# Seven half products for output tiles 0 and 1 in the steady cycles of a fused attention and MLP-mixer kernel

## The chip, the cores and the metric

The kernel runs on one core of a Trainium2 chip. Its engines work side by side, each through its own list of instructions in order: TensorE (PE, with its weight loads shown as PEld), VectorE (DVE), ScalarE (ACT), GpSimd (POOL) and SyncE (SP). DMAs are issued by SyncE, GpSimd and, in two places, ScalarE. The engines wait for one another through semaphores. The metric is the device time of one execution in microseconds; before and after are compared as medians of several runs.

## What is computed

```python
def _attn_ref(q, k, v):                      # q, k, v: 8 x 12 x 448 x 64
    scale = 1.0 / np.sqrt(q.shape[-1])
    scores = scale * np.matmul(q, k.transpose(0, 1, 3, 2)) - np.log(S)
    attn = 1.0 / (1.0 + np.exp(-scores))     # a sigmoid, no sum over keys
    return np.matmul(attn, v)

def _moe_ref(x, w_tok1, w_tok2, w_ch1, w_ch2):   # x: 8 x 448 x 768
    xt = x.transpose(0, 2, 1)
    h = np.maximum(xt @ w_tok1, 0.0) @ w_tok2    # 448 -> 256 -> 448, over tokens
    u = x + h.transpose(0, 2, 1)
    h2 = np.maximum(u @ w_ch1, 0.0) @ w_ch2      # 768 -> 1536 -> 768, over channels
    return u + h2                                # 8 x 448 x 768, fp32
```

The heads of the attention, side by side, are x. Everything is multiplied in fp16 and summed in fp32.

## The kernel before

A batch's twelve heads are handled as three *units* of four heads (u = 0, 1, 2), so that there are 24 *cycles*, c = 3b + u. In a cycle several stages of several batches stand side by side, in an order written out by hand (`tc.manual_schedule()`): what the Python program emits first stands first in each engine's list.

- *Scores*, `qk(b, u, j)` (L179): seven per unit. Four quarter products (64x64 weights, 448 columns) into a tile of two PSUM banks, then one sigmoid on ScalarE (L191). The tag `qk` has two such tiles, so the score after next waits for the sigmoid. The sigmoids' outputs `att` lie in ten buffers.
- *Values*, `av(b, u)` (L205), one cycle later: 28 quarter products into two banks; VectorE casts them to fp16 into `xTs[b % 2]` (L224), with a copy into the pad (L230). `xtrans_dma` (L239) then transposes x through a DMA on SyncE's queue into `xn`.
- *Token products*, `tok_tail`, `tok1` and `ytrans` (L264 to L333), two cycles later. `ytrans` ends with VectorE's add of x and the product into a tile of its own, `uts[b % 2]` (L323).
- In cycle 2 of batch b, `utrans(b - 1)` (L336) transposes u of the batch before through a DMA into `un`, `token_sums(b - 1)` forms four sums and differences of u (tile `diffs`), and `sevens(b - 1)` computes the first channel product as seven half products after Strassen and Winograd: `ORDER` (L1123) names each by its number and its column groups a, b, c, so that "5ab" is product 5 of groups a and b. They are accumulated in PSUM, and ScalarE moves some of them out to tiles of the ring `parts` (four buffers, L522 to L528); VectorE adds and clamps (L537, L540) into `h2`, of which there is one.
- *Second channel product* (`ch2...`), 448 tokens in four tiles (0 to 2 of 128 tokens, 3 of 64), two halves of 384 output channels, twelve blocks of 128 hidden channels. In cycle c of batch b it belongs to `lot` b - 2: `ch2_pair` for tile 0 in cycle 0 and tile 2 in cycle 2 (64 quarter and 8 full products each), and in cycle 1 `last_split` for tile 3 (48 quarters), `ch2_split` for the first half of tile 1 (48 quarters) and `ch2` for its second half (12 full). VectorE adds u from `un` into a tile `outs` (ring of three), which SyncE stores.
- `ch2_seven` (L723) does two output tiles at once by seven half products, six blocks each. It needs operand sums on both sides: `hsums`, sums of the weights `c2` made once by `output_sums` (L696, twelve VectorE instructions), and sums of `h2` per pair of tiles (`sums`, L750). Products 1, 6, 7 and 4 accumulate one after another in one bank ("X"), 5 and 3 in another; after each one VectorE adds the bank into the output tile (L790). Before the change it is used only in the last stage, for batches 6 and 7.
- `through_dma(b + 1)`: six VectorE copies (L126) and two DMA transposes (L139) bring the next batch's k and q into place; `some(n)` emits n of these pieces, `within` in the middle of a cycle and `behind` at its end. `gated_loads` issues the loads after next on GpSimd's queue, behind a copy that waits for the transposed q (L1048).

The loop of the steady cycles, L1209 to L1281, runs over b = 3 to 7. With "quarter" for a product of 64x64 weights and "full" for 128x128, its cycle reads, in TensorE's order:

```python
qk(b, u, 0); qk(b, u, 1); <quarters>; qk(b, u, 2)
av(*before, 0, 4); qk(b, u, 3); av(*before, 4, NJ); qk(b, u, 4)
<quarters>; qk(b, u, 5); <quarters>
tok_tail(*ahead); qk(b, u, 6); tok1(*ahead, with_scores=True)
<full products of ch2>; if u == 2: sevens(b - 1)
ytrans(*ahead)
```

Of the kernel before, what the change touches and what calls it, by code (L numbers as in the profile page):

```python
# [21 lines left out]
NJ = 7  # L22
NP = 64
NU = 3
# [6 lines left out]
def kernel(  # L31
# [44 lines left out]
    diffs = pc.tile([128, 4, NU, NS], FP16, name="diffs")  # L76
    xTs = [pc.tile([128, NU, 2, 512], FP16, name=f"xT{n}") for n in range(2)]

    uts = [pc.tile([128, NDB, 512], FP16, name=f"ut{n}") for n in range(2)]
# [125 lines left out]
    def av(b, u, j0=0, j1=NJ, banks=None):  # L205
        if j0 == 0:
            xa[b, u] = banks or [
                bank([128, 512], FP32, f"xa_{b}_{u}_{g}")
                for g in range(2)
            ]  # L210
        ps = xa[b, u]
        for j in range(j0, j1):
            for g in range(2):
                for hi in range(2):
                    nc.tensor.matmul(  # L215
                        out=ps[g][64 * hi : 64 * hi + 64, 0:S],
                        lhsT=raw[b, "v"][64 * g : 64 * g + 64, u, hi, j, :],
                        rhs=att[b, u, j][64 * g : 64 * g + 64, hi, :],
                        start=(j == 0),
                        stop=(j == NJ - 1),  # L220
                    )
        if j1 == NJ:
            for g in range(2):
                nc.vector.tensor_copy(  # L224
                    out=xTs[b % 2][:, u, g, 0:S], in_=ps[g][:, 0:S]
                )
            if NU * b + u >= N_CYCLES - 2:
                nc.vector.memset(xTs[b % 2][:, u, :, S:512], 0.0)
            elif NU * b + u >= N_FIRST:
                nc.vector.tensor_copy(  # L230
                    out=xTs[b % 2][:, u, :, S:512], in_=xTs[b % 2][:, u, :, S - 64 : S]
                )


    def xn_tile(b, u):
        xn[b, u] = pa.tile([128, 2, 4, 128], FP16, tag="xn", bufs=3, name=f"xn_{b}_{u}")
        return xn[b, u]

    def xtrans_dma(b, u):  # L239
        nc.sync.dma_start_transpose(  # L240
            out=xn_tile(b, u).rearrange("s g t d -> s (g t) d"),
            in_=xTs[b % 2][:, u, :, :].rearrange("d g s -> d (g s)"),
        )

    def xtrans(b, u):
        ps = bank([128, 4, 2, 128], FP16, f"xb_{b}_{u}")
        for g in range(2):
            for t in range(4):
                nc.tensor.transpose(
                    out=ps[:, t, g, :],  # L250
                    in_=xTs[b % 2][:, u, g, 128 * t : 128 * t + 128],
# [57 lines left out]
    def ytrans(b, u, banks=None):  # L309
# [11 lines left out]
        def add(g, ps):  # L321
            db = NU * g + u
            nc.vector.tensor_tensor(  # L323
                out=uts[b % 2][:, db, 0:S], in0=xTs[b % 2][:, u, g, 0:S], in1=ps[:, 0:S], op=ADD
            )
# [10 lines left out]
    def utrans(b):  # L336
        if b < B - 1:
            nc.vector.tensor_copy(
                out=uts[b % 2][:, 0:NU, S:512], in_=uts[b % 2][:, NU:NDB, S - 64 : S]
            )  # L340
        un[b] = pa.tile([128, NDB, 4, 128], FP16, tag="un", bufs=2, name=f"un_{b}")
        nc.sync.dma_start_transpose(
            out=un[b].rearrange("s db t d -> s (db t) d"),
            in_=uts[b % 2].rearrange("d db s -> d (db s)"),
# [6 lines left out]
    BY_UNIT = [NU * g + u for u in range(NU) for g in range(2)]  # L351

    def ch1(b, cb, d0=0, d1=NDB):
# [5 lines left out]
        for d in range(d0, d1):  # L359
# [3 lines left out]
                rhs=uts[b % 2][:, BY_UNIT[d], 0:S],  # L363
# [27 lines left out]
    def ch1_pair(b, cb):  # L391
# [3 lines left out]
        def step(turn, n):  # L395
# [7 lines left out]
                lambda p, part: uts[b % 2][part, BY_UNIT[n], 0:S],  # L403
# [34 lines left out]
    def token_sums(b, u0=0, u1=NU):  # L438

        ut = uts[b % 2]  # L440
        k1, k2 = slice(u0, u1), slice(NU + u0, NU + u1)
        n1, n2 = slice(0, NS), slice(NS, S)
        t1, t2, t3, t4 = (diffs[:, n, u0:u1, :] for n in range(4))
        for out, in0, in1, op in (
            (t1, ut[:, k1, n2], ut[:, k1, n1], SUB),
            (t3, ut[:, k2, n2], ut[:, k1, n2], SUB),
            (t2, t3, ut[:, k1, n1], ADD),
            (t4, ut[:, k2, n1], t2, SUB),
# [3 lines left out]
    def ch1_seven(b, banks):  # L452
# [3 lines left out]
        ut = uts[b % 2]  # L456
        s1, s2, s4 = sums
        low, high = slice(0, NU), slice(NU, NDB)
        n1, n2 = slice(0, NS), slice(NS, S)
        weights = {  # L460
# [9 lines left out]
            1: ut[:, low, n1],  # L470
            2: ut[:, high, n1],
            3: ut[:, high, n2],
            4: diffs[:, 3, :, :],
            5: diffs[:, 0, :, :],
            6: diffs[:, 1, :, :],
            7: diffs[:, 2, :, :],
# [71 lines left out]

    def ch2(b, t, half, n0=0, n1=NCB):
        cols = slice(DH * half, DH * half + DH)  # L550
        if n0 == 0:
            if half == 0:
                outs[b, t] = pa.tile([128, D], FP32, tag="outs", bufs=3, name=f"o_{b}_{t}")
# [12 lines left out]
        if b not in un:  # L566
            for n in range(NU):
                nc.tensor.matmul(
                    out=ps[:, 128 * n : 128 * n + 128],
                    lhsT=uts[b % 2][:, NU * half + n, 128 * t : 128 * t + 128],  # L570
# [6 lines left out]
    def ch2_out(b, t, half, ps):  # L577
        cols = slice(DH * half, DH * half + DH)
        if b in un:
            nc.vector.tensor_tensor(  # L580
                out=outs[b, t][:, cols].rearrange("s (u d) -> s u d", d=128),
                in0=un[b][:, NU * half : NU * half + NU, t, :],
# [5 lines left out]
        if half == 1:  # L588
# [9 lines left out]
    def ch2_pair(b, t):  # L598


        outs[b, t] = pa.tile([128, D], FP32, tag="outs", bufs=3, name=f"o_{b}_{t}")
# [47 lines left out]
    def ch2_split(b, t, half):  # L649

        outs[b, t] = pa.tile([128, D], FP32, tag="outs", bufs=3, name=f"o_{b}_{t}")
# [3 lines left out]
        def end():  # L655
            ch2_out(b, t, half, ps[0])
            o = outs[b, t][:, cols]
            nc.vector.tensor_tensor(out=o, in0=o, in1=ps[1][:, 0:DH], op=ADD)

# [9 lines left out]
    def last_split(b, ps):  # L669

        def end():
            o = pa.tile([128, DH], FP32, tag="outl", bufs=1, name=f"o_{b}_3")
# [3 lines left out]
                in0=un[b][:, 0:NU, 3, :],  # L676
# [19 lines left out]
    def output_sums():  # L696

        for tag in ("raw_k", "raw_q", "rel_k", "rel_q"):
            n = len(hsums) + 1
            hsums.append(  # L700
                pa.tile([128, NCB // 2, DH], FP16, tag=tag, bufs=1, name=f"hsum{n}")
            )
# [20 lines left out]
    class ch2_seven:  # L723
# [3 lines left out]
        def __init__(self, rows, sides, X, Y, Z):  # L727
            self.rows, self.ps, self.banks = rows, {}, {"X": X, "Y": Y, "Z": Z}
            b = rows[1][0]
            hid = pa.tile(  # L730
                [128, 3, NCB // 2, 128], FP16, tag="tr_k", bufs=2, name=f"hid_{b}"
            )
            hid3 = pa.tile([128, NCB // 2, 128], FP16, tag="tr_q", bufs=2, name=f"hid3_{b}")
            self.held = {n: hid[:, at, :, :] for at, n in enumerate((5, 6, 7))}
            self.held[3] = hid3[:, :, :]
            (self.a11, self.a12), (self.a21, self.a22) = [
                (side[:, LOW, :], side[:, HIGH, :]) for side in sides
            ]
            self.weights = {1: self.a11, 2: self.a12, 4: self.a22}
# [42 lines left out]

        def end(self, n):
            row, half = {1: (0, 0), 2: (0, 0), 6: (0, 1), 3: (0, 1)}.get(n, (1, int(n != 4)))
            b, t = self.rows[row]
            if (b, t) not in outs:
                outs[b, t] = pa.tile([128, D], FP32, tag="outs", bufs=3, name=f"o_{b}_{t}")
# [4 lines left out]
                in0=un[b][:, NU * half : NU * half + NU, t, :] if opens else o,  # L792
# [3 lines left out]
            if n in (3, 4):  # L796
                store(b, t)

    def ch2_last(b, n0=0, n1=NCB):
# [20 lines left out]
        for n in range(NU if add_on_pe else 0):  # L820
            for g in range(2):
                nc.tensor.matmul(
                    out=ps[g][:, 128 * n : 128 * n + 128],
                    lhsT=uts[b % 2][:, NU * g + n, 384:448],
# [4 lines left out]
        o = pa.tile([128, DH], FP32, tag="outl", bufs=1, name=f"o_{b}_3")  # L829
        for g in range(2):  # L830
# [4 lines left out]
            else:  # L835
                nc.vector.tensor_tensor(
                    out=o[parts[g], :].rearrange("s (u d) -> s u d", d=128),
                    in0=un[b][0:64, NU * g : NU * g + NU, 3, :],
# [30 lines left out]
    for n in range(2):  # L869
        nc.vector.memset(xTs[n][:, :, :, S:512], 0.0)  # L870
        nc.vector.memset(uts[n][:, :, S:512], 0.0)
# [254 lines left out]
    def sevens(b, banks=(2, 3, 0, 1, 0)):  # L1126
        step = ch1_seven(b, banks)
        for at, (n, gs) in enumerate(SEVENS):
            step(n, gs)
            if copies and at in (1, 3):  # L1130
# [77 lines left out]

    for c in range(ONE_RUN, N_CYCLES):  # L1209
        b, u = divmod(c, NU)  # L1210
        before, ahead = divmod(c - 1, NU), divmod(c - 2, NU)
        if b == NU:
            within, behind = ((0, 0), (3, 3), (2, 0))[u]
        else:
            within, behind = ((0, 2), (2, 4), (0, 0))[u] if b < B - 1 else (2, 2)
        if u == 0:
            assert not copies
            copies += through_dma(b + 1, 0) if b + 1 < B else output_sums()

        X, Y = 2, 0
        at_bank[0] = X
        if u == 1:
# [49 lines left out]
        if u == 2:  # L1274
            sevens(b - 1)
# [3 lines left out]
        if u == 1 and NU < b < B - 1:  # L1279
            gated_loads(b)  # L1280
# [38 lines left out]
    outs[B - 1, 2] = pa.tile([128, D], FP32, tag="raw_v", bufs=2, name=f"o_{B - 1}_2")  # L1319
# [57 lines left out]
```

## Time and profile before

| | |
|---|---|
| time, median of 3 runs | 344.02 us (343.84 to 344.08) |
| the profiled execution | 344.08 us, of which the profiled span is 342.3 us |
| granted TensorE clock, mean | 0.999 |
| busy: TensorE / VectorE / ScalarE / GpSimd | 335.2 / 219.1 / 214.3 / 56.7 us |
| batches 3 to 6 of the steady loop | 38.92 us each |
| output stores on SyncE's queue | 48 of 192 KB, 3.5 us to landing; 15 of 96 KB, 2.5 us |
| transposes on SyncE's queue, to landing | xn 3.5, tr_k 5.8, tr_q 6.5, un 9.3 us |

A line of the chain of waits gives a start in the span, a length, and the work that held the end of the kernel there, with the number of instructions merged into it. A line of the timeline gives the same for every engine, with the idle time ahead of it and what ended that in brackets. A line of the groups gives the busy time in all, the mean of one in ns, and the idle time of the engine before them. The output of a matmul is reported with a modelled end; a matmul overlaps its successor, so that a group's mean (some 320 ns for 384 columns) is longer than the time from one to the next. The line of the batches comes from the chain: the piece `PE c L383` that opens cycle 0 starts at 102.26, 141.19, 180.11, 219.03 and 257.95.

### The profile page before, as it was taken

Reading aid. Unit: us, or ns where it says so; the run is one execution under the profiler, and the core shown is the slowest. Engines: PE = TensorE matmul, PEld = TensorE weight load, DVE = VectorE, ACT = ScalarE, POOL = GpSimd, SP = SyncE. Lnnn points to the kernel's source line nnn. Section 1 sums busy time; section 2 is a strip of 40 time slices with the busy share of each in tenths; the row PEclk is TensorE's granted clock in tenths of the full one; section 3 lists DMA queues with packets and bytes.
Section 4 is the critical chain, followed back from the end, with each engine's and each line's share of the span. In section 5 each row is a group of like instructions: output and inputs, shape, how many; then the busy total and the mean of one; then the engine's idle time right before and its main releaser. Section 6 shows DMA issues by size and latency. Waiting matters only on the chain.

```text
span 342.3 us, 10437 instructions
## 1 busy us (share of the span) xinstructions
PE 335.2 (98%) x4543; PEld 238.9 (70%) x4543; DVE 219.1 (64%) x441; ACT 214.3 (63%) x272; POOL 56.7 (17%) x98
## 2 busy tenths in 40 slices
PE   7999999999999999999999999999999999999994
PEld 4556556555896669766896669766896669869862
DVE  2277466678774684666764674667655785876782
ACT  3997747388748785677648875577748876314200
POOL 8973440050040004000040004000100000000000
PEclk9999999999999999999999999999999999999999
DMA  7999999999999999998999599977991429029007
GB/s 124 164 177 194 207 204 204 157 170 177 243 170 209 161 141 202 193 172 133 184 189 187 113 181 168 226 127 137 188 191 33 100 57 163 2 54 181 7 6 201
DMA packets 104380, 52.17 MB, mean 152 GB/s; under 512 B 76432, under 2 KB 101264, under 8 KB 104336
## 3 DMA queue, kind: packets, MB, share of 16 engines
q1 hardware_dynamic: 78944, 29.70, 48.3%
q0 software_dynamic: 25168, 21.50, 41.6%
q8 instruction: 35, 0.57, 0.7%
q10 hardware_dynamic: 224, 0.33, 0.4%
q14 instruction: 9, 0.07, 0.1%
HBM read 43.45 MB, written 11.01 MB: 159 GB/s over the span
## 4 chain that ended last, share of the span: by engine, by line
PE 91%; ACT 5%; DMA 1%; DVE 1%; issue 1%; ACTq 0%; DVEq 0%
PE c_ab L507 14%; PE qk L184 10%; PE c_c L507 8%; PE c L383 8%; PE xa L215 8%; PE c L557 6%; PE c L772 6%; PE c L639 6%; PE tk L293 5%; PE yt L313 5%; ACT att L191 5%; PE c L621 4%; PE c L360 3%; DMA first_q<-in_q_dram 1%; PE c L811 1%; PE c_a L507 1%
## 5 line engine op out<-in xcount | busy, mean ns | idle before, releaser
L191 ACT ACTIVATE att<-qk,att_bias 128x896 f16<-128x896 f32 x168 | 157.2, 1014 | 42.2 <-PE qk L184 41.8
L184 PE MATMUL qk<-tr_q,tr_k 64*64 64x448 f16 x672 | 58.1, 360 | 0.3
L507 PEld LDWEIGHTS <-c 128*128 128x128 f16 x504 | 48.4, 98 | 1.1 <-issue 0.3
L224 DVE CAST xT<-xa 128x448 f16<-128x448 f32 x46 | 26.6, 619 | 29.7 <-PE xa L215 29.7
L215 PE MATMUL xa<-att,raw_v 64*64 64x448 f16 x644 | 38.0, 349 | 0.0
L507 PEld LDWEIGHTS <-sum 128*128 128x128 f16 x378 | 36.3, 98 | 0.0
L184 PEld LDWEIGHTS <-tr_k 64*64 64x64 f16 x672 | 20.1, 105 | 19.8 <-issue 11.9
L383 PE MATMUL c<-c,h 64*64 64x384 f16 x640 | 31.1, 322 | 0.0
L528 ACT ACTIVATE pt_ab<-c_ab 128x896 f32<-128x896 f32 x21 | 19.3, 917 | 18.6 <-PE c_ab L507 18.0
L580 DVE TENSOR_TENSOR o<-un,c 128x384 f32<-128x384 f16 x30 | 16.6, 554 | 20.8 <-PE c L621 10.2
L215 PEld LDWEIGHTS <-raw_v 64*64 64x64 f16 x672 | 20.2, 107 | 10.9 <-issue 0.4
L1048 POOL COPY gate<-tr_q 128x2 f16<-128x2 f16 x6 | 1.1, 186 | 154.6 <-DMA tr_q<-rel_q 154.6
L323 DVE TENSOR_TENSOR ut<-xT,yt 128x448 f16<-128x448 f16 x44 | 25.2, 614 | 1.7 <-PE yt L313 1.7
L383 PEld LDWEIGHTS <-h 64*64 64x64 f16 x640 | 18.7, 107 | 7.9
L557 PE MATMUL c<-c,h 128*128 128x384 f16 x132 | 24.1, 326 | 0.0
L639 PE MATMUL c<-c,h 64*64 64x384 f16 x480 | 22.1, 322 | 0.0
L530 ACT ACTIVATE h<-c_ab 128x896 f16<-128x896 f32 x7 | 6.4, 917 | 24.4 <-PE c_ab L507 24.4
L537 DVE TENSOR_TENSOR h<-pt_ab,c_ab 128x896 f16<-128x896 f32 x14 | 15.2, 1083 | 9.5 <-PE c_ab L507 9.5
L293 PE MATMUL tk<-xn,w 128*128 128x256 f16 x156 | 21.2, 274 | 0.1
L537 DVE TENSOR_TENSOR h<-pt_c,c_c 128x448 f16<-128x448 f32 x21 | 12.9, 616 | 12.6 <-PE c_c L507 12.6
L313 PE MATMUL yt<-w,h 128*128 128x448 f16 x88 | 20.3, 353 | 0.0
L639 PEld LDWEIGHTS <-h 64*64 64x64 f16 x528 | 15.4, 107 | 6.7
(118 smaller groups left out, 496.3 us busy)
## 6 DMA issues: line engine op xcount, KB each, us to landing
out_dram<-o SPq DMA_DIRECT2D x48, 192.0 KB, 3.5
c<-in_moe_w_ch_dram POOLq DMA_DIRECT2D x4, 1152.0 KB, 15.5
raw_k<-in_k_dram POOLq DMA_DIRECT2D x10, 336.0 KB, 9.0
raw_q<-in_q_dram POOLq DMA_DIRECT2D x10, 336.0 KB, 13.8
raw_v<-in_v_dram POOLq DMA_DIRECT2D x10, 336.0 KB, 10.8
out_dram<-o SPq DMA_DIRECT2D x15, 96.0 KB, 2.5
raw_q<-in_q_dram POOLq DMA_DIRECT2D x12, 112.0 KB, 5.3
raw_k<-in_k_dram POOLq DMA_DIRECT2D x12, 112.0 KB, 5.4
```

The costliest lines, as they stand in the source:

```text
L184: nc.tensor.matmul(out=ps[64 * g : 64 * g + 64, hi, 0:S], lhsT=tr[b, "k"][64 * hi : 64 * hi + 64, u, j, 64 * g : 64 * g + 64], rhs=tr[b, " ...
L191: nc.scalar.activation(out=att[b, u, j][:, :, :], in_=ps[:, :, 0:S], func=SIGMOID, bias=bias_t[:, :], scale=att_scale,)
L215: nc.tensor.matmul(out=ps[g][64 * hi : 64 * hi + 64, 0:S], lhsT=raw[b, "v"][64 * g : 64 * g + 64, u, hi, j, :], rhs=att[b, u, j][64 * g : ...
L224: nc.vector.tensor_copy(out=xTs[b % 2][:, u, g, 0:S], in_=ps[g][:, 0:S])
L293: nc.tensor.matmul(out=ps[tcb], lhsT=w1[rows, t, cols], rhs=xn[b, u][rows, :, t, :], start=(t == 0 and not with_scores), stop=(t == (2 if ...
L313: nc.tensor.matmul(out=ps[:, 0:S], lhsT=h1[b, u][:, tcb, g, :], rhs=w2[:, tcb, :, :], start=(tcb == 0), stop=(tcb == 1),)
L323: nc.vector.tensor_tensor(out=uts[b % 2][:, db, 0:S], in0=xTs[b % 2][:, u, g, 0:S], in1=ps[:, 0:S], op=ADD)
L383: nc.tensor.matmul(out=ps[p][m : m + 64, 0:n], lhsT=lhsT(p, part, m), rhs=rhs(p, part), start=(first and turn == 0), stop=(last and turn = ...
L507: nc.tensor.matmul(out=ps[:, g, p, :], lhsT=weights[n][:, d, 128 * cb : 128 * cb + 128], rhs=moving[n][:, d, :], start=(n in (1, 5, 2) and ...
L537: nc.vector.tensor_tensor(out=shaped(dst), in0=shaped(parts[gs, which]), in1=ps, op=ADD)
L557: nc.tensor.matmul(out=ps[:, 0:DH], lhsT=h2[b][:, BY_GROUP[cb], 128 * t : 128 * t + 128], rhs=c2[:, BY_GROUP[cb], cols], start=(cb == 0), ...
L639: nc.tensor.matmul(out=ps[r][m : m + 64, 0:DH], lhsT=lhsT(part, n, m), rhs=rhs(part, n, m), start=(n == 0), stop=(n == n_cb - 1),)
```

## The change

Batches 4 to 7 (lots 2 to 5) leave the old cycle for a new one, `steady(b, u)`; batch 3 keeps the old one.

- Output tiles 0 and 1 of a lot go through `ch2_seven`: products 1 and 2 in cycle 0 as quarters side by side (`two_jobs`, each group of four holds two quarters of either product), then 6 and 5 as full products; products 7 and 3 as quarters in cycle 1, then 4 full. Tile 2 has its first half as full products in cycle 1 and its second as quarters in cycle 2; tile 3 moves to cycle 2.
- Scores are taken in their order, six in cycle 0, six in cycle 1 and nine in cycle 2, instead of seven in each.
- `ytrans` adds in place: u replaces x in one tile `xu(b)` of [128, unit, half, 512] (batch 0 has a tile of its own), and `utrans`, `token_sums` and the channel products read it there. `uts` goes.
- Memory: output tiles 0, 1 and 3 come from the ring `parts`; only tile 2 uses `outs`, now of two. `xn` has two buffers instead of three. `diffs` becomes a tile with one buffer that `ch2_seven` shares for its sums in the steady cycles; its fourth sum overwrites a part of `h2`. The sums of `c2` have tiles of their own, shared with batch 0's, and the output tiles of batches 6 and 7 take the places of raw and rearranged k and q.
- `output_sums` moves from batch 7 to batch 3: four of its instructions at the start of cycle 0, three at that of cycle 1, five among the products of `sevens` in cycle 2.
- Of the pieces of `through_dma`, one is emitted at the end of cycle 0, three within cycle 1 and four behind it (before: two, two, four).

The core of the diff (`out_tile` and `last_tile` pick the tags just named; uses of `uts` and `xTs` become `xu` or `ut(b, db)`):

```diff
-            db = NU * g + u
-            nc.vector.tensor_tensor(
-                out=uts[b % 2][:, db, 0:S], in0=xTs[b % 2][:, u, g, 0:S], in1=ps[:, 0:S], op=ADD
-            )
+            x = xu(b)[:, u, g, 0:S]
+            nc.vector.tensor_tensor(out=x, in0=x, in1=ps[:, 0:S], op=ADD)
...
+    def two_jobs(jobs, n_quads):
+        def step(turn, n):
+            for r in range(2):
+                ps, lhsT, rhs, count, opens, end = jobs[r ^ turn]
+                part = slice(64 * r, 64 * r + 64)
+                for m in (0, 64):
+                    nc.tensor.matmul(
+                        out=ps[m : m + 64, 0:DH],
+                        lhsT=lhsT(n)[part, m : m + 64],
+                        rhs=rhs(n)[part, :],
...
+        def rest():
+            for ps, lhsT, rhs, count, opens, end in jobs:
...
+                end()
+        turns = [[lambda t=t, n=n: step(t, n) for n in range(n_quads)] for t in range(2)]
+        return turns[0] + turns[1], rest
...
+    def steady(b, u):
+        lot, before, ahead = b - 2, divmod(NU * b + u - 1, NU), divmod(NU * b + u - 2, NU)
+        within, behind = ((0, 1), (3, 4), (0, 0))[u]
...
+        if u < 2:
+            if u == 0:
+                sides = [h2[lot][:, :, 128 * t : 128 * t + 128] for t in range(2)]
+                sevenfold[lot] = ch2_seven(
+                    [(lot, 0), (lot, 1)], sides, X, X + 1, X + 1, at_end=False
+                )
+                sevenfold[lot].sums(0, 2)
+            seven = sevenfold[lot]
+            steps, end = two_jobs([seven.job(n) for n in ((1, 2), (7, 3))[u]], NCB // 2)
+            score(2)
+            run(steps, 6)
+            score()
+            at_bank[0] = Y
+            av(*before, 0, 4)
+            score()
+            av(*before, 4, NJ)
+            xtrans_dma(*before)
+            score()
+            run(steps, 6)
+            end()
+            if u == 0:
+                seven.sums(2, 4)
+            score()
+        else:
+            at_bank[0] = X
+            ps = [bank([128, 512], FP32, f"c2_{lot}_3_{r}") for r in range(2)]
+            steps, end = last_split(lot, ps)
+            score(2)
+            run(steps, NCB // 2)
+            score()
+            run(steps, NCB // 2)
+            end()
+            score()
+            at_bank[0] = Y
+            av(*before, 0, 4)
+            score()
+            av(*before, 4, NJ)
+            xtrans_dma(*before)
+            utrans(b - 1)
+            token_sums(b - 1)
+            score()
+            at_bank[0] = X
+            steps, end = ch2_split(lot, 2, 1)
+            run(steps, NCB // 2)
+            score()
+            run(steps, NCB // 2)
+            end()
+            score()
+        some(within)
+        at_bank[0] = Y
+        tok_tail(*ahead)
+        if u == 2:
+            score()
+        tok1(*ahead, with_scores=True)
+        if u == 0:
+            seven.plain(6)
+            seven.plain(5)
+        elif u == 1:
+            seven.plain(4)
+            at_bank[0] = X + 1
+            ch2(lot, 2, 0)
+        else:
+            sevens(b - 1)
+        at_bank[0] = Y
+        ytrans(*ahead)
+        some(behind)
+        if u == 1 and b < B - 1:
+            gated_loads(b)
```

## The prediction

> **What bounds the kernel now.** I read the page first (busy time, then the chain that ended last), then that chain in order of time through one steady batch, then the timeline of the other engines in the same stretch, then the groups by shape. The page:
>
> ```profile
> span 342.3 us, 10437 instructions
> PE 335.2 (98%) x4543; PEld 238.9 (70%) x4543; DVE 219.1 (64%) x441; ACT 214.3 (63%) x272; POOL 56.7 (17%) x98
> PE 91%; ACT 5%; DMA 1%; DVE 1%; issue 1%; ACTq 0%; DVEq 0%
> ```
>
> TensorE is busy 98% and holds 91% of the chain. A busy PE may still hide waits, because matmul ends are modelled, so I follow the chain through cycle 1 of batch 5 (start us, length us, what):
>
> ```profile
> 187.91 0.50 PE qk L184 x8
> 188.41 1.95 PE c L639 x48
> 190.36 0.19 PE qk L184 x4
> 190.55 0.76 PE xa L215 x16
> 191.30 0.19 PE qk L184 x4
> 191.49 0.57 PE xa L215 x12
> ...
> 194.69 0.76 PE tk L293 x6
> 195.45 1.95 PE c L557 x12
> 197.40 0.76 PE yt L313 x4
> 198.16 0.50 PE qk L184 x8
> ```
>
> Each piece begins where the one before ends: no wait. Two rows give the price of a product. Twelve full 128x128 products of 384 columns take 1.95 us, 0.1625 each; 48 quarter products (64*64) take 1.95 us too, so four run side by side and a group of four also costs 0.1625. I call either a slot. The chain is equally tight through batches 4 to 7: 180.11, 219.03 and 257.95 begin the same L383 piece, 38.92 us apart. Slots saved there are time saved, unless a new wait appears. The other engines in cycle 2 of the same batch, and three shapes of VectorE:
>
> ```profile
> 198.58 6.40 ACT L191 ACTIVATE att<-qk,att_bias 128x896 f16<-128x896 f32 x7 [2.23 <-PE qk L184]
> 201.70 1.16 DVE L224 CAST xT<-xa 128x448 f16<-128x448 f32 x2 [1.06 <-PE xa L215]
> 200.75 4.66 SPq L139 DMA_TRANSPOSE tr_q<-rel_q  x1
> 207.36 0.19 POOL L1048 COPY gate<-tr_q 128x2 f16<-128x2 f16 x1 [32.76 <-DMA tr_q<-rel_q]
> ```
>
> ```profile
> L790 DVE TENSOR_TENSOR o<-un,c 128x384 f32<-128x384 f16 x12 | 6.5, 550 | 1.5 <-PE c L772 1.5
> L790 DVE TENSOR_TENSOR o<-o,c 128x384 f32<-128x384 f32 x9 | 5.0, 551 | 1.5 <-PE c L772 1.5
> L707 DVE TENSOR_TENSOR hsum<-c x6: 548/550/552, 258.4 to 277.8; 128x768 f16<-128x768 f16 x6
> ```
>
> Seven sigmoids of 1.01 us (L191's mean is 1014 ns) fill 6.40 us, so in a run they start (6.40-1.01)/6 = 0.90 apart. VectorE idles before its casts; an add in place costs what another add does; SyncE's queue is held 4.66 us by the transpose of tr_q.
>
> **The change, part by part.**
>
> *Products removed.* Per batch of output, before: tile 0 and tile 2 by 64 quarters and 8 full products each, tile 1 by 48 and 12, tile 3 by 48: 224/4 + 28 = 84 slots. After: tiles 0 and 1 together by seven half products of six slots (four of them as 96 quarters, three as 18 full), tile 2 by 48 quarters and 12 full, tile 3 by 48: 192/4 + 30 = 78. Six slots at 0.1625 are 0.975 us, over lots 2 to 5 it is 3.90 us, on the path. No product changes its shape.
>
> *Changes between quarter and full products.* Two scores that open a cycle after full products take 0.50 against 2 x 0.19: 0.12 us for the change. The new order makes it three times a batch, as the old one does: 0.
>
> *Scores 6, 6, 9.* The scores buffer has two slots, so score n waits for the sigmoid of n-2. From the cycle's first score, the sigmoids begin at 0.36 (187.91 to 188.27 in the timeline) to 0.42 (198.16 to 198.58). The third ends at 0.36 + 2 x 0.90 + 1.01 = 3.17 to 3.23; some 0.04 later PE goes on (in the opening a sigmoid ends at 44.11 and the score behind it starts at 44.15). In new cycles 0 and 1 only six groups of four stand ahead of the third score, and PE reaches the fifth at 0.50 + 0.975 + 0.19 + 0.76 + 0.19 + 0.57 = 3.185 (before: 3.51 after eight groups). Wait 0.03 to 0.09; I take 0.05, in two cycles of four batches: 0.40 us lost. Bounds: 0, since a wait can't save time, or 0.26 each (2.1 us) if sigmoids ran end to end at 1.01. In cycle 2 the ninth score is reached at 6.96 against 6.87, the first channel product at 7.91 against 7.77, and product 2a at 9.06, when the token evictions behind the ninth sigmoid free its bank at about 8.95: all clear, by little. Behind a waiting score stand the value products, and behind those the casts and everything of the cycle.
>
> *VectorE.* Three more adds (12 against 9) and four operand sums per batch, 7 x 0.55 = 3.9 us, on an engine at 64%. The first two sums begin 1.0 us into cycle 0, after the previous adds (218.39 + 1.15 - 218.53), and end at 2.1; the casts come at 3.2. What PE waits for: products 1, 6, 7 and 4 accumulate in one bank, each behind VectorE's read of the sum before. In cycle 0 the casts and the pad copy end at 4.6, the adds of products 1 and 2 at 5.15 and 5.7; PE reaches product 6 at 4.45 + 0.19 + 0.11 + 0.76 = 5.5 and product 5 at 6.5. In cycle 1 the adds of 7 and 3 end at the same 5.15 and 5.7, against product 4 at 5.5 and tile 2 at 6.5. Hidden by 0.35 us at the closest; the cost if that cover goes is a rival below.
>
> *Output sums in batch 3 instead of 7.* Twelve at 0.55 us. Four stand ahead of cycle 0's casts (1.0 + 2.2 = 3.2 against 183.15 - 179.61 = 3.5), three in cycle 1 (done by 2.65, its next bank needed at 4.3), five among the channel products, where VectorE idles (9.2 + 12.6 + 9.5)/7 = 4.5 us a batch waiting at L537. PE waited for none of them in batch 7, so that batch gains nothing: 0.
>
> *Memory and queues.* Adding u into x makes the adder wait for the transpose that read x, which the token products had to wait for already: 0. Two xn buffers instead of three are freed a cycle early: 0. Output tiles in the ring of four make the eviction of product 5ab wait until tile 3 has been stored. That store is now queued in cycle 2 behind tr_q, whose issue ends at 205.41, 7.25 into the cycle; with 1.1 us of issue and 2.5 to 3.5 to landing (page, part 6) it lands by 12, and 5ab ends at 7.91 + 1.15 + 1.73 + 2.30 = 13.1. Behind it xn and un move 1.1 us: xn lands near 210, read at 223; un near 217, read at 223 too. The loads on POOL keep their gate: 0.
>
> *Sum.* -3.90 + 0.40 = -3.50 us. The span goes from 342.3 to 338.8. The profiled run took 344.08, 1.78 more than its span; with the median, 344.02, the forecast is 340.5.
>
> **Rivals.**
>
> 1. *ScalarE paces the scores.* If in the new bursts sigmoids start 0.95 apart, the fifth score waits 0.14 twice and the ninth 0.22: 0.5 a batch, 344.02 - 3.90 + 2.0 = 342.1. For it: the margins of 0.1 in cycle 2, which now holds nine scores and the channel evictions. Against it: the runs of seven at 0.90.
> 2. *VectorE becomes the pacer* (the other side). If VectorE reaches the adds late, or product 6 waits for all that stands behind the add, the two sums of products 7 and 3 included, it starts at 6.7 instead of 5.5; product 4 likewise behind two relayouts at 6.8 instead of 5.5. That is 1.2 + 1.3 = 2.5 a batch, 10 in all: 344.02 - 3.50 + 10.0 = 350.5. It decides from 0.35 us of lateness, and the kernel is slower from 0.35 + 0.45 in each of the two cycles. For it: four chained products in a bank. Against it: idle before the casts (1.06), and in the last stage the same chain of L772 products runs 84 in 13.65 us, 0.1625 each, with no wait.
> 3. *The ring holds ScalarE.* If the store of tile 3 lands 2.4 us after 13.1, the eviction of 5ab waits, and the channel products with it, for at most that in each batch: 344.02 - 3.50 + 9.6 = 350. For it: the store stands right behind the transpose of tr_q, which lands 9.2 into the cycle (POOL's copy that waits for it runs at 207.36), and the loads that this copy lets go start then. Against it: landing and use are still some 1 to 4 us apart. The Trainium skill, "DMA: Bandwidth & Descriptors", section "Queues, rings and completion order", says that a DMA engine reports a transfer only after every earlier write of that engine, from whichever queue. By this rule the store cannot be reported before tr_q has landed, and a load ahead of it could push it further; no run here shows such a wait yet.
> 4. *The change doesn't do what it says*: the quarters of two different products do not run four at a time, or the time comes back at the next gate. Half of the 24 groups lost in cycle 1 alone, at 0.08 each, eats the saving: 344. Against it: L383 already runs quarters of two output halves into two banks at 1.30 us for 32, 0.1625 a group.
>
> **How the numbers follow.** Forecast 0.70 (340.5; its own range 339.9, with waits of nearly nothing, to 341.3), rival 1 0.14 (342.1), rival 4 0.05 (344), rival 2 0.07 and rival 3 0.04 (350). A measurement of this kernel tells 0.2%, 0.7 us, from no change. Forecast and rival 1 lie below 343.3: faster 0.84; rival 4: same 0.05; rivals 2 and 3: slower 0.11. The range runs from 339.9 to 342.7, past rival 1 with 0.6 us for margins lost on the path; the cases at 344 and 350 stay out.
>
> **What would show it.** 120 matmuls fewer (4423). Batches 4 to 7 at 38.0 us each (38.92 less 0.975, plus 0.1), with batch 3 still at 38.92. In cycles 0 and 1 a chain that touches ScalarE for under 0.1 us before the fifth score, and nowhere an add of the seven products. If rival 1 holds, sigmoid pieces stand in the chain of cycle 2; if rival 2, adds on products 6 and 4; if rival 3, evictions that wait for a DMA. A batch above 38.4 us, or lost time outside batches 4 to 7, would make the prediction wrong.

## The result, and the profile after

Five runs of the changed kernel have a median of 348.02 us (347.81 to 350.51), five of the kernel before 344.0 us (343.54 to 344.08). The ratio is 1.014 with an interval of 1.0105 to 1.0175: the change costs 4.0 us, where the prediction had 3.5 us gained. The profiled run took 347.81 us.

The page of the changed kernel, its first lines and the chain's shares by engine:

```profile
span 346.0 us, 10264 instructions
PE 334.9 (97%) x4423; PEld 242.7 (70%) x4423; DVE 232.3 (67%) x467; ACT 213.4 (62%) x272; POOL 56.7 (16%) x98
PE 85%; DMA 7%; ACT 5%; DVE 1%; issue 1%; DVEq 0%; ACTq 0%
```

The 120 matmuls are gone, and yet TensorE is busy as long as before (334.9 us against 335.2). DMA has gone from 1% of the chain to 7%. So there are two things to find: a wait for a transfer, and time that is booked as busy TensorE though fewer products are made.

Where the time lies by batch comes from the chain again: the piece of quarters that opens cycle 0 (from batch 4 on L848, two products side by side). The starts are at 100.85, 139.77, 178.61, 222.66 and 261.57; the third is read off the timeline, since the chain runs over a DMA there. The batch 7 column ends at the first piece of the last stage, at 296.38 before and 299.98 after.

| us | start of batch 3 | batch 3 | 4 | 5 | 6 | 7 | rest |
|---|---|---|---|---|---|---|---|
| before | 102.26 | 38.93 | 38.92 | 38.92 | 38.92 | 38.43 | 45.9 |
| after | 100.85 | 38.92 | 38.84 | 44.05 | 38.91 | 38.41 | 46.0 |
| predicted | 102.26 | 38.92 | 38.05 | 38.05 | 38.05 | 37.55 | 45.9 |

The opening scatters between executions of all kernels (that start lies between 100.85 and 102.32 in seven of the eight profiles shown here, at 104.47 in the last), so the 1.4 us by which it is shorter here are none of the change. Batch 5 lost 5.1 us. Batches 4, 6 and 7 gained 0.08, 0.01 and 0.02 of the 0.87 us that each should have gained.

**Batch 5.** The chain of the changed kernel, in the stretch before and behind the DMA:

```profile
167.07 0.55 PE c_b L512 x6
167.62 18.75 DMA un<-xu
...
186.49 0.56 DVE o L832
...
187.10 2.93 PE c L804 x12
190.03 1.49 PE yt L315 x4
```

The transpose of u into `un` took 18.75 us from issue to landing, where the page before had a median of 9.3. VectorE's first add of u (L832) starts on its landing, and product 6 (L804), which goes into the bank that this add reads, starts behind it. The timeline puts the price on it:

```profile
167.62 12.63 SPq L342 DMA_TRANSPOSE un<-xu  x1
186.49 0.55 DVE L832 TENSOR_TENSOR o<-un,c 128x384 f32<-128x384 f16 x1 [3.57 <-DMA un<-xu]
187.10 2.93 PE L804 MATMUL c<-hsum_a,hid 128*128 128x384 f16 x12 [3.28 <-DVE o L832]
```

TensorE stood 3.28 us. The pieces after it are slow as well: twelve full products took 2.93 instead of 1.95 us, four of `yt` 1.49 instead of 0.76. The table of windows of the same kernel (columns: busy time and count of PE, PEld, DVE, ACT, POOL, then the granted clock, the DMA share and GB/s) shows why:

```profile
183.00:186.00 3.00, 0.82 (x10) 0.59 (x7) 0.00 (x0) 1.59 (x4) 0.00 (x0) 1.00 0.98 140
186.00:189.00 3.00, 1.90 (x10) 1.11 (x10) 2.48 (x5) 0.00 (x0) 0.00 (x0) 0.87 0.64 186
189.00:192.00 3.00, 3.00 (x20) 1.13 (x22) 1.65 (x4) 0.04 (x1) 0.00 (x0) 0.56 0.01 3
192.00:195.00 3.00, 3.00 (x68) 2.00 (x64) 0.76 (x3) 3.00 (x4) 0.00 (x0) 1.00 0.03 5
```

After the idle stretch the granted clock was 0.56 for some 3 us (in windows of 0.25 us it is 0.50 from 188.25 to 191.50). That adds 0.98 + 0.73 = 1.71 us; with the 3.28 it makes 4.99 of the 5.1.

What made the transfer late stands in the order of SyncE's queue and GpSimd's, in batch 4 (timeline of the changed kernel, first SyncE's rows, then GpSimd's with the copy that lets the loads go):

```profile
160.50 3.95 SPq L141 DMA_TRANSPOSE tr_q<-rel_q  x1
164.56 1.18 SPq L711 DMA_DIRECT2D out_dram<-o  x2
165.85 1.25 SPq L242 DMA_TRANSPOSE xn<-xu  x1
167.62 12.63 SPq L342 DMA_TRANSPOSE un<-xu  x1
```

```profile
166.43 0.19 POOL L1121 COPY gate<-tr_q 128x2 f16<-128x2 f16 x1 [31.57 <-DMA tr_q<-rel_q]
166.97 1.32 POOL L117 DMA_DIRECT2D raw_k<-in_k_dram  x2 [0.35 <-issue]
```

Tile 3's two stores (L711) now stand between tr_q and xn. They hold up xn and un, but not the loads of the next q, k and v, which wait for tr_q alone. Before the change, in batches 3 to 6, un was issued 1.0 to 2.7 us ahead of the first load; here it comes 0.65 us behind it, and even its issue lasts 12.63 us. The two rows in batch 5 of the kernel before:

```profile
206.86 4.36 SPq L342 DMA_TRANSPOSE un<-ut  x1
207.90 1.31 POOL L115 DMA_DIRECT2D raw_k<-in_k_dram  x2 [0.35 <-issue]
```

**The other batches.** Batch 6, cycle 0, then the start and the end of cycle 2 in the chain of the changed kernel:

```profile
222.16 0.50 PE qk L186 x8
222.66 0.97 PE c L848 x24
223.64 0.33 PE qk L186 x4
223.97 0.76 PE xa L217 x16
224.72 0.19 PE qk L186 x4
224.91 0.57 PE xa L217 x12
225.48 0.28 PE qk L186 x4
...
240.33 0.97 PE c L665 x24
241.31 0.38 PE qk L186 x4
...
247.00 0.28 PE qk L186 x4
...
248.06 1.31 PE c_ab L512 x12
249.37 0.60 PE c_a L512 x6
```

There is no gap between these pieces but 0.01 to 0.02 us of issue, and no other engine; the wait is inside the lengths. A score after quarters or values takes 0.19 us. Here the third takes 0.33 and the fifth 0.28, in cycle 0 and again in cycle 1: (0.14 + 0.09) x 2 = 0.46. In cycle 2 the third takes 0.38 behind 0.01 of issue (0.20), the ninth 0.28 (0.09), and the first channel products 1.31 behind 0.02 of issue instead of 1.15 (0.18) and 0.60 instead of 0.57 (0.03): 0.50. Together 0.96 us a batch, against 0.975 saved. The list of waits for this stretch has no line of TensorE's products, since the records of matmuls overlap and so show no idle time here. The timeline of ScalarE and TensorE in cycle 0 shows them:

```profile
222.53 5.50 ACT L193 ACTIVATE att<-qk,att_bias 128x896 f16<-128x896 f32 x6 [0.54 <-PE qk L186]
223.59 0.38 PE L186 MATMUL qk<-tr_q,tr_k 64*64 64x448 f16 x4
224.53 0.39 PE L186 MATMUL qk<-tr_q,tr_k 64*64 64x448 f16 x4
225.38 0.38 PE L186 MATMUL qk<-tr_q,tr_k 64*64 64x448 f16 x4
```

Six sigmoids in 5.50 us are (5.50 - 1.01)/5 = 0.90 apart, so the first three end at 223.54, 224.44 and 225.34. The third and the fifth score need the first and the third of these, and their records start 0.05 and 0.04 later. The fourth needs the second sigmoid, which is long done: its record starts at 224.53, 0.19 before the piece ahead of it ends in the chain (224.72). That is the normal overlap. So a product that starts 0.05 after its release, instead of 0.19 before its turn, loses 0.24 less its margin, the margin being the time from the release to the end of the piece ahead. The four scores that waited fit (the first channel product, too, starts 0.05 behind its release: the eighth sigmoid ends at 247.00 + 1.01 = 248.01, the product's record starts at 248.06):

| score | sigmoid it needs ends | piece ahead ends | margin | 0.24 - margin | lost |
|---|---|---|---|---|---|
| third, cycle 0 | 223.54 | 223.64 | 0.10 | 0.14 | 0.14 |
| fifth, cycle 0 | 225.34 | 225.48 | 0.14 | 0.10 | 0.09 |
| third, cycle 2 | 241.26 | 241.30 | 0.04 | 0.20 | 0.20 |
| ninth, cycle 2 | 246.84 | 247.00 | 0.16 | 0.08 | 0.09 |

### The profile page after: what moved, and what is told of

Read it like the earlier page. It is cut to its first block, busy times and chain, and to the rows that moved or that the text cites. A ratio compares the mean times of both kernels' runs of the same rounds, so it can differ in the third digit from the quotient of the medians.

```text
span 346.0 us, 10264 instructions
## 1 busy us (share of the span) xinstructions
PE 334.9 (97%) x4423; PEld 242.7 (70%) x4423; DVE 232.3 (67%) x467; ACT 213.4 (62%) x272; POOL 56.7 (16%) x98
## 4 chain that ended last, share of the span: by engine, by line
PE 85%; DMA 7%; ACT 5%; DVE 1%; issue 1%; DVEq 0%; ACTq 0%
PE c_ab L512 13%; PE qk L186 10%; PE c L804 10%; PE xa L217 7%; PE c_c L512 7%; PE c L583 6%; PE c L665 6%; DMA un<-xu 5%; PE tk L295 5%; ACT att L193 5%; PE yt L315 5%; PE c L848 4%; PE c L363 3%; PE c L386 2%; DMA first_q<-in_q_dram 1%; PE c L885 1%
## 5 line engine op out<-in xcount | busy, mean ns | idle before, releaser
L186 PE MATMUL qk<-tr_q,tr_k 64*64 64x448 f16 x672 | 59.2, 359 | 0.6 <-ACT att L193 0.2
L226 DVE CAST xu<-xa 128x448 f16<-128x448 f32 x40 | 23.1, 620 | 24.8 <-PE xa L217 24.8
L186 PEld LDWEIGHTS <-tr_k 64*64 64x64 f16 x672 | 23.4, 105 | 23.2 <-issue 16.1
L217 PEld LDWEIGHTS <-raw_v 64*64 64x64 f16 x672 | 22.5, 107 | 8.1 <-issue 0.4
L533 ACT ACTIVATE pt_ab<-c_ab 128x896 f32<-128x896 f32 x21 | 19.3, 917 | 13.2 <-PE c_ab L512 12.6
L665 PE MATMUL c<-c,h 64*64 64x384 f16 x480 | 23.0, 322 | 0.0
L325 DVE TENSOR_TENSOR xu<-xu,yt 128x448 f16<-128x448 f16 x38 | 21.9, 615 | 0.3 <-PE yt L315 0.2
L832 DVE TENSOR_TENSOR o<-un,c 128x384 f32<-128x384 f16 x28 | 15.3, 552 | 8.1 <-PE c L804 4.6
L665 PEld LDWEIGHTS <-h 64*64 64x64 f16 x528 | 17.3, 107 | 4.8
L309 ACT ACTIVATE h<-tk 128x256 f16<-128x256 f32 x42 | 14.0, 397 | 9.5 <-PE tk L295 9.5
L804 PEld LDWEIGHTS <-hid 128*128 128x128 f16 x120 | 11.9, 99 | 11.1 <-issue 4.0
## 6 DMA issues: line engine op xcount, KB each, us to landing
raw_q<-in_q_dram POOLq DMA_DIRECT2D x10, 336.0 KB, 14.4
```

Source lines behind the costliest of these rows:

```text
L186: nc.tensor.matmul(out=ps[64 * g : 64 * g + 64, hi, 0:S], lhsT=tr[b, "k"][64 * hi : 64 * hi + 64, u, j, 64 * g : 64 * g + 64], rhs=tr[b, " ...
L217: nc.tensor.matmul(out=ps[g][64 * hi : 64 * hi + 64, 0:S], lhsT=raw[b, "v"][64 * g : 64 * g + 64, u, hi, j, :], rhs=att[b, u, j][64 * g : ...
L226: nc.vector.tensor_copy(out=xu(b)[:, u, g, 0:S], in_=ps[g][:, 0:S])
L325: nc.vector.tensor_tensor(out=x, in0=x, in1=ps[:, 0:S], op=ADD)
L665: nc.tensor.matmul(out=ps[r][m : m + 64, 0:DH], lhsT=lhsT(part, n, m), rhs=rhs(part, n, m), start=(n == 0), stop=(n == n_cb - 1),)
L804: nc.tensor.matmul(out=ps[:, 0:DH], lhsT=self.weights[n][:, k, :], rhs=self.moving[n][:, k, :], start=(n in (1, 2, 5) and k == 0), stop=(k ...
```

## The experiments

Two theories were to be separated from rivals: A, that batch 5's loss is un coming behind the loads; C (so called in the expectations), that the rest of the missing gain is scores, and the first channel product, too close behind their sigmoids.

**e1, the stores behind un.** The changed kernel, with tile 3's stores issued behind xn and un. Since tile 3 then lives longer, it comes from `outs` and not from the ring.

```diff
     def last_tile(b):
+        if NU - 1 <= b < B - 2:
+            return pa.tile([128, DH], FP32, tag="outs", bufs=2, name=f"o_{b}_3")
...
+            if NU - 1 <= b < B - 2:
+                held_back.append(stores)
+            else:
+                stores()
...
             xtrans_dma(*before)
             utrans(b - 1)
+            held_back.pop()()
             token_sums(b - 1)
```

> Tile 3's two stores (lots 2 to 5) stand behind un's transpose on SyncE's queue, from a tile of the outs ring; all else as changed. Theory A (the stores pushed un behind the loads that tr_q's landing lets go): un's transposes of batches 4 to 6 land within 12 us of their issue (18.75 and 13.2 before), TensorE no longer waits for un (3.3 us, and 1.7 us at half clock behind it), batch 5 takes 38.9 us instead of 44.05, and the time falls by 5 us, to about 343. Theory A says nothing of the 0.95 us that each batch lost beside: batches 4 to 7 stay at 38.9. Rival B (un is slow because the faster loop's transfers collide whatever their order): un still lands after 13 to 19 us in one of the batches, and the time stays near 348.

Measured: 344.05 us (343.61 to 346.42, ten runs) beside 344.42 for the kernel before (342.73 to 345.23, nineteen runs); ratio 1.0, interval 0.998 to 1.0019. In its timeline un is issued at 167.82 and the first load at 168.77; un lands in 9.9 us, the others in batches 5 and 6 in 11.1 and 9.5, and no batch waits for it. Batches 4 to 7 are 38.91 us. The loss of batch 5 is gone with the order of the queue. The "about 343" of the expectation is missed by 1 us: it took 5 us off the 348 of the changed kernel, whose profiled run had its opening 1.4 us shorter than this one (100.85 against 102.30).

**e2, the loads behind un.** The same end by the other queue: the stores stay where they are, and the copy that lets the loads go waits for xn instead of tr_q and is emitted after `utrans`.

```diff
         nc.gpsimd.tensor_copy(
-            out=gate[:, :], in_=tr[b + 1, "q"][:, NU - 1, NJ - 1, 126:128]
+            out=gate[:, :],
+            in_=tr[b + 1, "q"][:, NU - 1, NJ - 1, 126:128] if behind is None else behind,
         )
...
             utrans(b - 1)
+            if b < B - 1:
+                gated_loads(b, xn[before][:, 1, 3, 126:128])
...
-        if u == 1 and b < B - 1:
-            gated_loads(b)
```

> The stores stay where the change put them; GpSimd's loads wait for the landing of xn instead of tr_q (issue of both just ahead of un), so they start some 3 us after un's issue. Theory A: un again lands within 12 us of its issue, no wait of TensorE for un, about 343 us as with the stores moved. Rival B: no difference, 348. A third way: the later loads make the next batch's rearranged k or the values late, above 348.

Measured: 344.0 us (343.02 to 348.81, ten runs), ratio 1.0012, interval 0.9979 to 1.0045. Two of the ten runs took 347.99 and 348.81 us; why is open, since neither is the profiled one. In the profiled run (343.91 us) the first load of batch 4 is issued at 173.10, 4.1 us behind un (2.7 and 4.1 in batches 5 and 6), and the three uns land in 6.0, 7.8 and 6.2 us, faster than any un of these batches in the kernels with the old gate (9.1 at the least). Batches 4 to 7 are 38.91. Two edits with nothing in common but the order of un and the loads remove the same loss, so the stores as such (their bytes, their place in the ring) are not its cause.

**b1, the same order in the kernel before.** Nothing of the change but the place of the stores: tile 3 is computed where it was, and its stores are held back to cycle 2, behind tr_q.

```diff
+            if b < B - 2:
+                held_back.append(stores)
+            else:
+                stores()
...
             qk(b, u, 2)
             some(within)
+            if u == 2:
+                held_back.pop()()
```

> The kernel before, with tile 3's stores issued one cycle later: behind tr_q, ahead of xn and un, where the change put them. Theory A: un's issue slips behind the loads in one or more of batches 3 to 6, with 13 to 19 us to landing instead of 8 to 11.5. The old cycle reads un 1.4 us later in cycle 0 than the new one, so the loss is smaller: up to 2 us where un takes 18.75, 0 where it takes 13; 344.0 to 346. Rival B: un's landing stays at 8 to 11.5 us and the time at 344.0.

Measured: 354.99 us (352.12 to 356.96), ratio 1.0307, interval 1.0238 to 1.0376. The direction was expected, the size is far above the expected one, which was 2 us at most. Two pieces of its chain, with what follows the second:

```profile
131.47 21.97 DMA un<-ut
...
215.05 20.68 DMA un<-ut
...
235.85 0.57 DVE o L580
...
236.46 3.90 PE c L639 x37
```

Two of the four uns fall behind the loads and cost 7.55 and 4.28 us. TensorE stood 5.39 and 2.34 us of it; most of the rest is the 48 quarters behind the wait (a few of their records are missing), which took 4.10 and 3.90 us instead of 1.95, at a granted clock of 0.50 up to 157.5 and 239.5. Whether un is overtaken is a matter of tenths of a microsecond, as ten of the uns of these kernels show when they are put in the order of their lead (issue of the first load less issue of un; from the timelines of SyncE and GpSimd):

| kernel | un issued | lead over the first load | issue lasts | issue to landing |
|---|---|---|---|---|
| e2 | 168.99 | 4.11 | 4.38 | 6.0 |
| before | 206.86 | 1.04 | 4.36 | 10.1 |
| e1 | 167.82 | 0.95 | 4.84 | 9.9 |
| b1 | 176.77 | 0.62 | 3.83 | 10.7 |
| after | 212.00 | 0.56 | 3.87 | 11.9 |
| b1 | 257.55 | 0.28 | 4.32 | 14.4 |
| after | 251.03 | -0.13 | 9.86 | 13.2 |
| b1 | 215.05 | -0.32 | 13.36 | 20.7 |
| b1 | 131.47 | -0.46 | 12.62 | 22.0 |
| after | 167.62 | -0.65 | 12.63 | 18.75 |

With half a microsecond of lead un lands in 10 to 12 us, with a third of one or more behind in 19 to 22. In the rows at 257.55 and 251.03 (batch 6) only the two loads of v follow, in the others six loads, so these two rows are not a pure matter of lead. Nor does more lead always help: at 2.70 us in batch 4 of the kernel before un took 11.3. A's part is settled by e1, e2 and b1 together.

**e3, how many products ahead of a score.** On e1, with another order in each batch: none, one, two or three value blocks (0.19 us each) moved ahead of the third score in cycles 0 and 1, and six, seven, eight or nine groups ahead of the third score of cycle 2.

```diff
+        first, second, third, n1 = {4: (0, 4, 0, 6), 5: (1, 4, 0, 7), 6: (2, 5, 0, 8), 7: (3, 6, 0, 9)}[b]
...
             run(steps, 6)
+            at_bank[0] = Y
+            if first:
+                av(*before, 0, first)
             score()
...
-            run(steps, NCB // 2)
+            run(steps, n1)
             score()
-            run(steps, NCB // 2)
+            run(steps, NCB - n1)
```

> On top of the moved stores, the work between scores varies by batch: in batches 4, 5, 6, 7 the third score of cycles 0 and 1 stands behind 0, 1, 2, 3 value blocks and the fourth behind 4, 4, 5, 6; in cycle 2 the third score stands behind 6, 7, 8, 9 groups. Theory C (a score's wait must clear about 0.25 us before TensorE gets there, since the weight loads of its other quarters stand behind the waiting matmul): in cycle 2 the third score's piece costs 0.38, then 0.2 to 0.3, then 0.19, 0.19, with margins to the first sigmoid's end of about 0.05, 0.2, 0.37, 0.53; in cycles 0 and 1 the loss moves from the third score to the fifth, and the sum of both stays near 0.23. Rival D (plain lateness: the loss is what the sigmoid's end exceeds TensorE's arrival): the third score's piece costs 0.19 wherever the sigmoid ends first, in all four batches of cycle 2 alike.

Measured in one run: 343.96 us, span 342.2. Lines of its chain, in order of time: the third score of cycle 2 in batch 4, the fifth score of cycle 0 in batch 6, and the third score of cycle 2 in batch 6:

```profile
159.89 0.38 PE qk L186 x4
...
221.61 0.38 PE qk L186 x4
...
237.86 0.19 PE qk L186 x4
```

In cycle 2 the third score takes 0.38, 0.23, 0.19 and 0.19 us with six to nine groups ahead of it, 0.16 us apart: the loss falls with the margin and is nothing from two more groups on, as C has it. By rival D the third score would have lost nothing even with six or seven groups, since its sigmoid ends 0.04 and 0.20 us ahead of its turn. In cycles 0 and 1 nothing is won: the score that is moved back is whole again, but the later ones come no later than they did, and with two blocks the fifth takes 0.38 behind 0.04 of issue, 0.23 too much, which is the third's 0.14 and the fifth's 0.09 together. Batches 4, 5, 6 and 7, measured from the first scores, are 38.91, 38.75, 38.73 and 39.03 us. Three blocks are too many: there the chain runs over the sigmoids themselves.

**e4, shorter sigmoids.** On e1, the sigmoids of batches 4 to 7 work on 320 of 448 columns, and the value products read 224 of them twice, so that no matmul changes its shape. A part of the attention is left out.

```diff
+        n = S - 128 if b > NU else S
         nc.scalar.activation(
-            out=att[b, u, j][:, :, :],
-            in_=ps[:, :, 0:S],
+            out=att[b, u, j][:, :, 0:n],
+            in_=ps[:, :, 0:n],
...
-                        rhs=att[b, u, j][64 * g : 64 * g + 64, hi, :],
+                        rhs=seen(att[b, u, j][64 * g : 64 * g + 64, hi, :], b),
```

> On top of the moved stores, the sigmoids of batches 4 to 7 take 320 of 448 columns of each half (640 in place of 896), and the value products read 224 of them twice, so that part of the attention is left out and TensorE's list of products stays as it is. Theory C (all of the 0.95 us that a batch lost is scores, and one channel product, that wait for sigmoids): with each sigmoid some 0.2 us shorter every margin exceeds 0.25, and batches 4 to 6 take 38.91 - 0.95 = 37.96 us, six slots below 38.92. Rival E (the half products, their adds or the moved tiles cost part of it): the batches stay above 38.3 with scores at 0.19 each.

Measured in one run: 340.84 us, span 339.1, 3.2 us less than e1's 342.3; 2.97 of it lie in batches 4 to 7. Lines of its chain from batch 5, cycle 0 and the end of cycle 2:

```profile
180.19 0.19 PE qk L186 x4
...
181.89 0.19 PE qk L186 x4
...
183.25 0.19 PE tk L280 x4
...
203.04 0.19 PE qk L186 x4
...
203.99 1.21 PE c_ab L516 x12
```

Every score is back at 0.19, and a batch takes 38.17 us: 0.74 of the 0.975 is there. That is above C's 37.96 and below rival E's 38.3. The 0.22 that is still missing shows in the same chain: the first token products take 0.19 instead of 0.11 in cycles 0 and 1, and the first channel product 1.21 instead of 1.15. Its timeline shows what holds them. The token products go into the banks of the values, and VectorE's second cast (L230) frees the second bank at 183.09, 0.16 ahead of the end of the piece before; by the rule of the scores 0.24 - 0.16 = 0.08 is lost, as it is. The channel product's record starts at 203.89, 0.05 behind the end of the eighth sigmoid. So not every margin exceeds 0.25 as the expectation had it: with the scores' waits gone, the next gates are 0.06 to 0.08 us away.

**e5, more products ahead in cycle 2.** On e1: eight groups ahead of the third score of cycle 2, `token_sums` behind tile 2's last quarters, and product 1c ahead of 1ab.

```diff
+    STEADY = [SEVENS[3], *SEVENS[:3], *SEVENS[4:]]
...
+        first, second, third, n1 = {b: (0, 4, 0, 8)}[b]
...
-            run(steps, NCB // 2)
+            run(steps, n1)
             score()
-            run(steps, NCB // 2)
+            run(steps, NCB - n1)
...
-            token_sums(b - 1)
+            held_back.pop()()
             score()
...
             end()
+            token_sums(b - 1)
             score()
...
-            sevens(b - 1)
+            sevens(b - 1, order=STEADY)
```

> On top of the moved stores, cycle 2 of batches 4 to 7 is rearranged alone: eight groups instead of six ahead of its third score, the token sums behind the last quarters of tile 2, and the channel products begin with 1c, so that 1ab stands 0.57 us further from the eighth sigmoid. Theory C: the third score loses 0 instead of 0.19, 1ab 0 instead of 0.18, 2a 0 instead of 0.03, the ninth score still 0.09 and cycles 0 and 1 still 0.23 each, perhaps 0.05 to 0.1 for 6ab behind the eviction of 1ab: 38.5 to 38.6 us a batch, 1.2 to 1.6 us below the kernel before, 342.5 to 343 beside 344.0. If the loss only moves on inside cycle 2, 38.9 a batch and 344.

Measured: 342.7 us (341.52 to 346.63, twelve runs) beside 343.95 for the kernel before (342.78 to 345.52, seventeen runs); ratio 0.9981, interval 0.9951 to 1.0011. Its chain at the end of cycle 2:

```profile
200.91 0.19 PE qk L186 x4
...
206.10 0.28 PE qk L186 x4
...
207.14 0.57 PE c_c L512 x6
207.72 1.15 PE c_ab L512 x12
```

The third score and the channel products are whole, the ninth score still loses 0.09, and the sixth loses a new 0.03. A batch takes 38.55 us, 0.37 below 38.92: 1.5 us over four batches, as its profile shows and the medians (1.25) agree, though the interval does not exclude that nothing is gained (the profiled run itself took 344.87, since it opens 2.2 us later than that of the kernel before). Its median is the lowest of the versions that compute everything. That 1ab is freed fits the order of 1c: the eighth sigmoid, which releases 1ab's tile, ends at 207.11, and 1ab starts at 207.55. What the later token sums add was not tried alone. Cycles 0 and 1 still lose 0.23 each; the fifth score could not be moved further back in this scheme, because the two halves of `two_jobs` stand on both sides of it, and another arrangement wasn't tried.

## Why the prediction was wrong

- *Products removed*: right. There are 4423 matmuls, and with short sigmoids the batch falls by 0.74 us, with the missing 0.22 visible elsewhere in the chain. Of the gain itself next to nothing came (0.01 to 0.08 us a batch), for the reasons below.
- *Changes between quarter and full products*, *Output sums in batch 3*: right at nothing. The two scores that open a cycle take 0.50 as before; batch 3 takes 38.92.
- *VectorE*: right. The one add on the chain is the one that waited for un; with un on time (e1) there is none, so rival 2 did not come about. What has no term in it is that the casts of the values become the next gate, for 0.08 us twice a batch, once the scores no longer wait (e4).
- *Scores 6, 6, 9*: wrong, and the first step that failed. The prediction gave a score 0.04 us of need behind its sigmoid and found the fifth short by 0.05, the rest "all clear, by little". The mechanism was right and the size was not: the need is 0.24 us, since a product that waits also loses the 0.19 by which it would have overlapped the one ahead. The term was 0.10 us a batch; it measured 0.46 in cycles 0 and 1, and cycle 2, priced at nothing with margins of 0.09 and 0.14, lost 0.50. The third score was not looked at, though it had the smallest margins of all: six groups ahead of it instead of eight or more took away at least 0.33 us.
- *Memory and queues*: wrong, and dearer. "Behind it xn and un move 1.1 us" was short: from the end of tr_q's issue to un's it took 1.45 to 1.47 us before and 2.75 to 3.33 after, so un moved 1.3 to 1.9. "The loads on POOL keep their gate" was right; the step that failed is to put the landing of un at 217 from this, with its usual 9 to 10 us. The two queues move against each other: un was moved and the loads were not, and the time that a transfer takes hangs on which of the two comes first. It needed 18.75 us, TensorE stood 3.28, and with the clock that made 5.1. The prediction shows the copy at 207.36; un's issue, at 206.86 in the same profile, was not set against it: a lead of half a microsecond over the copy and of 1.04 over the first load, less than even the 1.1 of shift.
- Rival 1 (ScalarE paces the scores, 0.5 a batch) had the right engine and half the size; the sigmoids did not stretch, they start 0.90 apart as in the forecast. Rival 4 had a total of 344 for "the time comes back at the next gate", which is what e1 measures, 344.05. The other half of rival 4 did not come about: 24 quarters of two products take 0.97 us, 0.1625 a group of four.
- Rival 3 (the ring holds ScalarE) did not come about: no eviction waits for a DMA in the chain or the timeline of the changed kernel. The Trainium skill's rule of "DMA: Bandwidth & Descriptors", section "Queues, rings and completion order", which stood beside it, is therefore borne out neither way here: no store landed late enough to be waited for.
- The clock was not in the working. The row is 0.56 granted over 3 us behind 3.28 us idle. The Trainium skill, "TensorE: Matmul & The Clock Gate", section "What's actually happening", says that an idle window of about 3.4 us halves the clock and that a busy one of that length restores it. The trace agrees in the second: the clock is at half for some 3.4 us, which makes the 1.71 measured. It does not agree in the first: 3.28 us of idle time were enough here, and 2.34 in b1.

Together: 5.1 us for un, and some 3.8 of the 3.9 us saved given back at waits of 0.03 to 0.20 us. With un in order the change makes no difference (e1), and where no score waits 2.97 us are gained in batches 4 to 7 (e4).

## What to carry to other kernels

Where TensorE is full, a margin is measured from the moment at which the next product would start to overlap, not from the end of the piece ahead: here a score's buffer has to be free 0.24 us before that end, and the loss shows as a piece that is longer than its like, not as a wait. Before a step is moved down one DMA queue, its new place is to be compared with what the other queues release, to tenths of a microsecond: a transfer that slips behind a bulk load is not late by the shift but by the load. And the clock comes on top of a stall of TensorE: stalls of 2.34, 3.28 and 5.39 us each cost another 1.7 to 2.2 us here, most of it at half the clock.

## What had not been expected of the hardware

A transpose issued 0.3 to 0.65 us behind the first of six loads took 12.6 to 13.4 us to issue and 18.75 to 22.0 to land; 0.5 to 1 us ahead of it, 3.8 to 4.8 and 10 to 12; with the loads held back to 2.7 to 4.1 us behind it (e2), 3.7 to 4.5 and 6 to 8. At a lead of -0.13 us, with two loads instead of six behind the gate, it was between, 9.86 and 13.2. Why a few tenths decide, when both queues have work for the next 10 us in either order, no run here shows.
